# Unread products between the groups of rows while the first batch loads, and from the first microsecond

## Chip, cores, metric

One core of one Trainium2 chip. The metric is the device time of one execution in microseconds (us). Beside it, each execution has a span, the time from its first to its last instruction, and a mean granted clock of TensorE. The time is usually 2.1 to 2.2 us more than the span.

## The reference

Four batches of 6016 rows and 256 columns. A cross-covariance attention over the columns is followed by a gated feed-forward layer:

```python
qn = q / (norm(q, axis=1) + 1e-6);  kn = k / (norm(k, axis=1) + 1e-6)
s = kn.transpose(0, 2, 1) @ qn / tau           # 256 x 256 per batch
a = softmax(s)                                 # with 1e-9 added to the sum
x = (v @ a).reshape(24064, 256)
out = (sigmoid(x @ w_gate) * (x @ w_val)) @ w_out   # d_ff = 1536
```

The scores and norms of a batch need all of its rows, so nothing of the first batch's output can start before all of q and k of that batch are loaded.

## The kernel before

While the first batch loads, TensorE works group by group (four tiles of 128 rows; at the end a group of two tiles and one of one): score products, then the norms of the group before, which multiply squares by a column of ones.

```python
    def busy(n):

        ps = psg.tile([P, CH], FP32, tag="g", name="ps_busy")
        for _ in range(n):
            mm(ps[:, :P], ones_bf, ones_bf, True, True)

    ps_n0 = psm.tile([P, 2 * CB], FP32, tag="m", name="ps_n")
    sq = {}
    last0 = len(groups0) - 1
    for g in range(last0 + 2):
        if g <= last0:
            t0, nt = groups0[g]
            sq[g] = (
                squares(0, t0, nt, 0, nc.vector),
                squares(0, t0, nt, 1, nc.vector if g == last0 else nc.scalar),
            )
            for u in range(nt):
                score(0, t0, u)
        if g >= 1:
            norm_mms(ps_n0, sq.pop(g - 1), groups0[g - 1][1], g == 1, g == last0 + 1)
    st[0]["n"] = ps_n0
    norms_sqrt(0)
    # ... cut ...
    norms_inv(0)          # VectorE: r = r + 1e-6, r = 1 / r   (128x4)
    copy_s(0, 1)
    busy(12)
    spread_k(0)           # TensorE: ps_rk, needs r
    busy(10)
    # ... cut: scale, exponential, sums, products with the weights; then the main loop
```

`busy` was there already: products that nobody reads, between the stages of the softmax.

## Time and profile before

| | before |
|---|---|
| time, median of 3 | 840.12 us (839.49 to 840.18) |
| span of the profiled execution | 838.0 us |
| mean granted clock | 0.992 |
| TensorE busy | 817.0 us, 97% |

TensorE's busy share is that of an engine at its limit almost throughout. The clock rows, the chain of waits and the timeline of the head, which is where the change acts, are shown in the prediction below. In the chain, each line is a start, a length and what held the end there; a DMA line is a transfer waited for. In the windows, the columns are the window, its length, the busy time of TensorE, its weight load, VectorE, ScalarE and GpSimd, then clock, DMA share and GB/s.

### The profile page before, as it was taken

Reading aid. Unit: us, or ns where it says so; the run is one execution under the profiler, and the core shown is the slowest. Engines: PE = TensorE matmul, PEld = TensorE weight load, DVE = VectorE, ACT = ScalarE, POOL = GpSimd, SP = SyncE. Lnnn points to the kernel's source line nnn. Section 1 sums busy time; section 2 is a strip of 40 time slices with the busy share of each in tenths; the row PEclk is TensorE's granted clock in tenths of the full one; section 3 lists DMA queues with packets and bytes.
Section 4 is the critical chain, followed back from the end, with each engine's and each line's share of the span. In section 5 each row is a group of like instructions: output and inputs, shape, how many; then the busy total and the mean of one; then the engine's idle time right before and its main releaser. Section 6 shows DMA issues by size and latency. Waiting matters only on the chain.

```text
span 838.0 us, 14001 instructions
## 1 busy us (share of the span) xinstructions
PE 817.0 (97%) x5338; PEld 506.6 (60%) x5338; DVE 566.3 (68%) x977; ACT 390.6 (47%) x640; POOL 83.2 (10%) x159
## 2 busy tenths in 40 slices
PE   5899999999999999999999999999999999999998
PEld 4646666665666666665565666666566556665666
DVE  2377777776667777777656777777756666666664
ACT  4554444445644444444554444444654444444442
POOL 5532100002011100000210020000000000000000
PEclk9799999999999999999999999999999999999999
DMA  9999624226655443223864453223222422322211
GB/s 209 206 205 186 124 51 89 61 51 136 125 102 107 101 102 63 54 51 85 153 132 83 92 118 80 51 73 67 60 48 51 95 51 73 78 50 65 49 36 69
DMA packets 78739, 77.18 MB, mean 92 GB/s; under 512 B 50769, under 2 KB 55633, under 8 KB 78673
## 3 DMA queue, kind: packets, MB, share of 16 engines
q0 software_dynamic: 23920, 38.81, 28.0%
q1 hardware_dynamic: 54608, 36.97, 15.8%
q8 instruction: 41, 0.67, 0.3%
q10 hardware_dynamic: 144, 0.52, 0.2%
q14 instruction: 26, 0.20, 0.1%
HBM read 78.64 MB, written 24.64 MB: 123 GB/s over the span
## 4 chain that ended last, share of the span: by engine, by line
PE 91%; DMA 3%; DVE 2%; ACT 1%; issue 1%; POOL 0%; ACTq 0%; POOLq 0%
PE ps_o L88 29%; PE ps_gate L88 28%; PE ps_val L88 28%; PE ps_s L88 4%; DMA k_sb<-in_k_dram 3%; PE ps_gh L88 2%; DVE hT L351 1%; ACT g_sb L350 1%; PE ps_rk L88 0%; DVE out_sb L377 0%; ACT gh_H L306 0%; PE ps_n L88 0%; DVE gh_H L308 0%; DVE gh_G L308 0%; DVE x_sb L253 0%
## 5 line engine op out<-in xcount | busy, mean ns | idle before, releaser
L351 DVE TENSOR_TENSOR hT<-ps_val,g_sb 128x512 bf16<-128x512 f32 (+1 forms) x576 | 391.1, 679 | 219.9 <-ACT g_sb L350 216.3
L350 ACT ACTIVATE g_sb<-ps_gate 128x512 bf16<-128x512 f32 (+1 forms) x576 | 338.8, 588 | 399.8 <-PE ps_gate L88 387.3
L88 PE MATMUL ps_val<-vT,gh_H 128*128 128x512 bf16 (+1 forms) x1152 | 338.0, 375 | 0.5
L88 PE MATMUL ps_gate<-vT,gh_G 128*128 128x512 bf16 (+1 forms) x1152 | 337.5, 375 | 0.0
L88 PE MATMUL ps_o<-w_out_sb,hT 128*128 128x256 bf16 x2256 | 326.2, 273 | 0.0
L88 PEld LDWEIGHTS <-hT 128*128 128x128 bf16 x2256 | 220.7, 98 | 124.8
L88 PEld LDWEIGHTS <-gh_H 128*128 128x128 bf16 x1152 | 112.7, 98 | 132.9 <-ACT gh_H L306 1.5
L88 PEld LDWEIGHTS <-gh_G 128*128 128x128 bf16 x1152 | 112.5, 98 | 37.4 <-ACT gh_G L306 0.3
L377 DVE COPY out_sb<-ps_o 128x256 f32<-128x256 f32 x188 | 78.1, 415 | 20.9 <-PE ps_o L88 20.9
L106 POOL DMA_DIRECT2D v_sb<-in_v_dram x48 | 25.6, 534 | 631.7 <-DMA vT<-v_sb 466.0
L88 PE MATMUL ps_s<-k_sb,q_sb 128*128 128x256 bf16 x376 | 72.4, 296 | 13.1 <-ACT k_sb L128 6.8
L88 PEld LDWEIGHTS <-q_sb 128*128 128x128 bf16 x376 | 39.1, 104 | 20.8 <-issue 7.1
L169 DVE TENSOR_TENSOR sq<-q_sb 128x1024 bf16<-128x1024 bf16 (+3 forms) x46 | 30.4, 661 | 20.7 <-PE ps_n L88 17.4
L207 DVE TENSOR_TENSOR acc<-acc,sq 128x1024 bf16<-128x1024 bf16 (+1 forms) x66 | 44.2, 669 | 0.0
L97 POOL DMA_DIRECT2D q_sb<-in_q_dram x48 | 26.4, 549 | 15.6 <-DMA q_sb<-in_q_dram 5.5
L97 POOL DMA_DIRECT2D k_sb<-in_k_dram x48 | 26.1, 545 | 13.6 <-DMA k_sb<-in_k_dram 8.4
L169 DVE TENSOR_TENSOR sq<-k_sb 128x1024 bf16<-128x1024 bf16 (+2 forms) x34 | 22.4, 658 | 0.0
L167 ACT ACTIVATE sq<-k_sb 128x1024 bf16<-128x1024 bf16 (+1 forms) x12 | 12.2, 1021 | 15.6 <-DMA k_sb<-in_k_dram 12.6
L88 PE MATMUL ps_gh<-w_gate,e_sb 128*128 128x512 bf16 x48 | 14.1, 378 | 1.6 <-DVE rrow L281 1.2
L88 PE MATMUL ps_gh<-w_val,e_sb 128*128 128x512 bf16 x48 | 14.1, 379 | 0.4
L88 PEld LDWEIGHTS <-e_sb 128*128 128x128 bf16 x112 | 9.9, 97 | 6.8 <-issue 3.2
L306 ACT ACTIVATE gh_G<-ps_gh,rrow 128x512 bf16<-128x512 f32 x12 | 8.2, 687 | 9.7 <-PE ps_gh L88 9.6
(46 smaller groups left out, 101.6 us busy)
## 6 DMA issues: line engine op xcount, KB each, us to landing
out_dram<-out_sb SPq DMA_DIRECT2D x44, 512.0 KB, 2.8
v_sb<-in_v_dram POOLq DMA_DIRECT2D x44, 256.0 KB, 3.9
q_sb<-in_q_dram POOLq DMA_DIRECT2D x43, 256.0 KB, 6.3
k_sb<-in_k_dram POOLq DMA_DIRECT2D x43, 256.0 KB, 7.8
out_dram<-out_sb SPq DMA_DIRECT2D x4, 384.0 KB, 2.4
w_gate<-in_moe_w_gate_dram POOLq DMA_DIRECT2D x3, 256.0 KB, 6.9
w_val<-in_moe_w_val_dram POOLq DMA_DIRECT2D x3, 256.0 KB, 7.6
w_out_sb<-in_moe_w_out_dram POOLq DMA_DIRECT2D x1, 768.0 KB, 12.6
```

The source lines that it names most:

```text
L88: nc.tensor.matmul(out, lhsT=lhsT, rhs=rhs, start=start, stop=stop, **kw)
L97: nc.gpsimd.dma_start(out=tl[:, :nt, :], in_=rows(src, b)[:, t0 : t0 + nt, :])
L106: nc.gpsimd.dma_start(out=v_sb[:, :nt, :], in_=rows(v, b)[:, t0 : t0 + nt, :])
L167: nc.scalar.activation(out=sq[:, :nt, :], in_=src[:, :nt, :], func=ACT.Square)
L169: engine.tensor_tensor(out=sq[:, :nt, :], in0=src[:, :nt, :], in1=src[:, :nt, :], op=ALU.mult)
L207: nc.vector.tensor_tensor(out=acc[:, :nt, :], in0=acc[:, :nt, :], in1=st[b]["sq", w][:, :nt, :], op=ALU.add)
L306: nc.scalar.activation(out=dst, in_=ps, func=ACT.Copy, scale=r)
L350: nc.scalar.activation(out=g_sb[:, :n], in_=ps_gate[:, :n], func=ACT.Sigmoid)
L351: nc.vector.tensor_tensor(out=hts[b, ci][:, f, :n], in0=ps_val[:, :n], in1=g_sb[:, :n], op=ALU.mult)
L377: nc.vector.tensor_copy(out=out_sb[:, s, :], in_=ps)
```

## The change

The intent: in the kernel before, TensorE's granted clock falls from 1.00 to 0.50 at times (18.37 and 28.61 us in the windows of the prediction), and the engine waits for loads during the first 31 us. Unread products fill these waits, so that the real ones run at full clock.

```diff
+    busy(40)
     ps_n0 = psm.tile([P, 2 * CB], FP32, tag="m", name="ps_n")
 ...
         if g >= 1:
             norm_mms(ps_n0, sq.pop(g - 1), groups0[g - 1][1], g == 1, g == last0 + 1)
+        if g < NT // TPC:
+            busy(12)
     st[0]["n"] = ps_n0
```

`NT // TPC` is 11: one filling after each group of four tiles.

## The prediction

> **What bounds the kernel now.** I read the page first, then the chain of waits of the first 60 us, then the timeline of TensorE, then windows.
>
> ```profile
> PE 91%; DMA 3%; DVE 2%; ACT 1%; issue 1%; POOL 0%; ACTq 0%; POOLq 0%
> PEclk9799999999999999999999999999999999999999
> ```
>
> The chain that ended last is TensorE for 91% of the span, and the granted clock is full in every slice of 21 us but the second. From 60 us on TensorE is simply full of work that the diff doesn't touch. So only the head, some 40 us, can move, and what the head saves should arrive at the end undiminished. The chain of waits in the head:
>
> ```profile
> 10.92 10.63 DMA k_sb<-in_k_dram
> ...
> 21.84 9.74 DMA k_sb<-in_k_dram
> 31.57 0.04 issue
> 31.61 1.86 PE ps_s L88 x8
> 33.48 0.40 PE ps_n L88 x16
> 33.88 0.88 PE ps_s L88 x4
> 34.76 0.40 PE ps_n L88 x16
> 35.16 0.43 PE ps_s L88 x2
> 35.59 0.28 PE ps_n L88 x12
> 35.87 0.69 PE ps_busy L88 x12
> ```
>
> Columns are start, length, what. Up to 31.57 us the head is paced by the loads of q and k, whose queue is full; TensorE waits for them. At 31.57 us group 10, the last group of four rows, is there, and from then on nothing waits for a load: 4.26 us of TensorE work lead to 35.87 us. That is all that a better clock could shorten. The timeline of TensorE has the same work at two speeds:
>
> ```profile
> 26.61 1.03 PE L88 MATMUL ps_s<-k_sb,q_sb 128*128 128x256 bf16 x8 [0.55 <-DMA k_sb<-in_k_dram]
> 27.48 0.54 PE L88 MATMUL ps_n<-ones_bf,sq 128*128 128x1 bf16 x16
> ...
> 31.61 1.86 PE L88 MATMUL ps_s<-k_sb,q_sb 128*128 128x256 bf16 x8 [0.20 <-DMA k_sb<-in_k_dram]
> 33.27 0.61 PE L88 MATMUL ps_n<-ones_bf,sq 128*128 128x1 bf16 x16
> 33.74 1.01 PE L88 MATMUL ps_s<-k_sb,q_sb 128*128 128x256 bf16 x4
> 34.55 0.61 PE L88 MATMUL ps_n<-ones_bf,sq 128*128 128x1 bf16 x16
> ```
>
> From start to start, eight score products take 27.48 - 26.61 = 0.87 us (109 ns each) in the fast state and 33.27 - 31.61 = 1.66 us (208 ns each) in the slow one. The sixteen one-column products of the norms take 0.47 us slow (33.74 - 33.27) and about 0.41 us fast: hardly clock-bound.
>
> In quarter-microsecond windows the clock drops at 18.37 us, rises at 25.20, drops at 28.61 and rises at 35.44. The distances are 6.83, 3.41 and 6.83 us, so I cut the head into windows of 3.41 us on that grid:
>
> ```profile
> 11.54:14.96 3.42, 2.37 (x45) 2.10 (x44) 1.12 (x2) 1.49 (x2) 1.33 (x3) 1.00 1.12 210
> 14.96:18.37 3.41, 1.56 (x26) 1.43 (x26) 0.95 (x2) 1.15 (x2) 1.33 (x3) 1.00 1.12 208
> 18.37:21.78 3.41, 2.19 (x26) 1.64 (x25) 0.69 (x1) 1.09 (x2) 1.06 (x2) 0.50 1.12 210
> 21.78:25.20 3.42, 3.14 (x30) 2.29 (x29) 0.69 (x1) 1.93 (x2) 1.59 (x3) 0.50 1.12 209
> 25.20:28.61 3.41, 2.27 (x44) 2.06 (x43) 1.31 (x2) 1.11 (x2) 1.51 (x3) 1.00 1.12 210
> 28.61:32.03 3.42, 2.68 (x27) 1.97 (x27) 0.77 (x2) 1.41 (x2) 1.67 (x4) 0.50 1.19 200
> 32.03:35.44 3.41, 3.41 (x46) 2.64 (x45) 0.88 (x3) 1.33 (x2) 3.33 (x6) 0.50 1.21 207
> ```
>
> The third column is TensorE's busy time, the clock is the third from the end. A window with 2.37 us busy was followed by a fast one, those with 1.56 and 2.27 us by a slow one; from the slow state 3.14 and 3.41 us led out, 2.19 and 2.68 us did not. The last window, slow, is the stretch that counts.
>
> **What the Trainium skill says.** "TensorE: Matmul & The Clock Gate", Part 1, "What's actually happening": the default is half clock, a free-running window of about 3.4 us decides, and a busy window gives the full clock. The grid of 3.41 us and the steps between 1.00 and 0.50 agree. Its table lets the clock fall after an idle window; here it fell after windows that were 46% and 66% busy, so partial activity counts. Same page, "Back-to-back issue gap": 256 columns should take 213 ns cold and 109 ns warm; the trace has 208 and 109. The clock row reads 1.00 before any product ran, but the first sixteen score products (start 6.84 us, norms at 10.21 us) took 211 ns each, so that reading is only what stood before the first record.
>
> **The change part by part.** Nothing is removed or moved.
>
> 1. Forty products of 128 columns at the start. Their operand is filled by VectorE at 0.84 to 1.01 us; TensorE has nothing before 6.84 us. At half clock I estimate 107 ns each (half of 213 ns): 4.3 us, to about 5.4 us. They end before the first group can start, so they cost nothing. They make the first groups fast, but those then wait for loads all the same: worth nothing at the end by itself.
> 2. Twelve products after each of the eleven groups of four. The chain has 0.69 us for twelve in the fast state. A group then needs 0.87 + 0.41 + 0.69 = 1.97 us of TensorE, while groups arrive about every 2.5 us (waits end at 26.61, 29.15, 31.61 us). So ten of the eleven fillings end before the next group, and cost nothing.
> 3. The clock. Busy share becomes about 1.97/2.5 = 79%, some 2.7 us of a window, against 2.37 us that held and 2.27 us that did not. Should it fall, a group needs 1.66 + 0.47 + 12 x 0.107 = 3.41 us, more than arrives in, so TensorE saturates and the clock comes back. I take it that the tail is fast.
> 4. The tail. From 31.61 us: eight scores 0.87, norms 0.41, the eleventh filling 0.69, four scores 0.44 (half of 0.87), so the next norms start at 34.02 us, not 34.55 us: 0.53 us earlier. Without the filling it would be 1.2 us; the last filling is on the path, and gives over half away. After that VectorE must square the last row once these norms free its buffer, then the last norms follow: a chain of about 1.1 us with little clock in it (0.03 to 0.1 us faster). Sum: 0.55 to 0.65 us.
>
> Loads don't stop it: k of group 11 was issued at 24.38 us and took about 8.5 us (32.9 us), of group 12 at 27.09 plus 6.5 us (33.6 us); the new times ask for them at 33.6 and 34.4 us. Nor do weights: the first value weight, issued at 30.61 us plus the page's 7.6 us, is there at 38.2 us, and is wanted at 39.3 us instead of 39.93 us. So 840.12 - 0.6 = 839.5 us.
>
> **Rivals.**
> - The clock falls again, and the tail is slow with a filling in it: 12 x 0.107 = 1.28 us more, 841.4 us. For it: 2.7 us busy is not far above the edge, and the grid's phase may differ between runs. Against it: saturation heals it. Some 8%.
> - The gain is hidden by a load: the arrival of a late group or the value weight takes the place of the slow products. The time stays at 840.1 us. Margins of 0.7, 0.8 and 1.1 us speak against it, 10%.
> - The kernel before is sometimes fast in its tail already (its runs go from 839.49 to 840.18 us, the profiled one was 840.19): then the gain in the median is smaller, but the new time is the same.
> - A large gain, above 2% (17 us): there is no such thing to win, since the slow windows cost only 4.26 us minus about 2.5 us where no load is waited for.
>
> **Range and chances.** The centre is 839.5 us. Spread of the runs (0.7 us), the first rival and the size of the tail's gain make it 838.8 to 840.3 us. All outcomes lie within 0.2% of before, so within 2% is 0.99.
>
> **What would show it right or wrong.** Clock 1.00 from the first filling's second window to 36 us. Eight scores of group 10 in about 0.87 us, starting at 31.6 us as before, since loads pace it. Twelve fillings of about 0.69 us directly ahead of group 11's scores. First square root near 35.3 us in place of 35.91 us, and the same lead at the end. It is wrong if group 10 arrives at another time, if the tail is slow, or if a wait for a load stands between 33 and 41 us.

## More of the kernel before

GpSimd issues all loads that change the type, in this order: q and k of the first batch, a tile of v, six weight tiles, a tile of v, the output weights.

## The result, and the profile after

| | before | after |
|---|---|---|
| time, median of 6 | 839.64 us (839.29 to 840.18) | 839.49 us (839.43 to 839.55) |
| span, profiled | 838.0 us | 837.4 us |
| mean clock, profiled | 0.992 | 1.00 |

The ratio is 0.9997, 95% interval 0.9985 to 1.001. A ratio is the mean time of one kernel's runs over that of the other's of the same rounds, so it is not quite the ratio of the medians quoted. The spread is a seventh of what it was: 0.12 us against 0.89 us.

The clock row of the page after, in 40 slices of the span:

```profile
PEclk9999999999999999999999999999999999999999
```

The 7 in the second slice has gone. The chain of waits of the changed kernel, from the last load:

```profile
21.88 9.73 DMA k_sb<-in_k_dram
31.61 0.04 issue
31.66 1.03 PE ps_s L88 x8
32.69 0.38 PE ps_n L88 x16
33.07 0.69 PE ps_busy L88 x12
33.76 0.44 PE ps_s L88 x4
34.20 0.38 PE ps_n L88 x16
34.58 0.24 PE ps_s L88 x2
34.82 0.41 PE ps_n L88 x12
35.22 0.69 PE ps_busy L88 x12
```

The load ends where it ended before, at 31.6 us. The eight scores now take half as long, the eleventh filling stands in the chain with 0.69 us, and the last norms end at 35.22 us, against 35.87 us. The first square root starts at 35.26 us instead of 35.91 us. So 0.65 us were gained in the profiled pair, and the span is 0.6 us shorter. Yet the medians of the same session differ by 0.15 us only. The experiments ask why.

### The profile page after: what moved, and what is told of

Read it like the earlier page. It is cut to its first block, busy times and chain, and to the rows that moved or that the text cites. A ratio compares the mean times of both kernels' runs of the same rounds, so it can differ in the third digit from the quotient of the medians.

```text
span 837.4 us, 14334 instructions
## 1 busy us (share of the span) xinstructions
PE 821.7 (98%) x5499; PEld 514.2 (61%) x5510; DVE 566.4 (68%) x977; ACT 390.4 (47%) x640; POOL 83.0 (10%) x159
## 4 chain that ended last, share of the span: by engine, by line
PE 91%; DMA 3%; DVE 2%; ACT 1%; issue 1%; POOL 0%; ACTq 0%; POOLq 0%
PE ps_o L88 29%; PE ps_gate L88 28%; PE ps_val L88 28%; PE ps_s L88 4%; DMA k_sb<-in_k_dram 3%; PE ps_gh L88 2%; DVE hT L351 1%; ACT g_sb L350 1%; PE ps_rk L88 0%; DVE out_sb L377 0%; ACT gh_H L306 0%; PE ps_n L88 0%; DVE gh_H L308 0%; DVE gh_G L308 0%; DVE x_sb L253 0%
## 5 line engine op out<-in xcount | busy, mean ns | idle before, releaser
L88 PE MATMUL ps_s<-k_sb,q_sb 128*128 128x256 bf16 x376 | 66.2, 272 | 6.1 <-DMA k_sb<-in_k_dram 4.4
L88 PEld LDWEIGHTS <-q_sb 128*128 128x128 bf16 x376 | 36.6, 98 | 12.1 <-issue 5.6
L97 POOL DMA_DIRECT2D q_sb<-in_q_dram x48 | 26.4, 550 | 16.6 <-DMA q_sb<-in_q_dram 7.3
L88 PE MATMUL ps_busy<-ones_bf 128*128 128x128 bf16 x194 | 14.7, 234 | 1.1 <-DVE shift L125 1.1
```

What stands on the lines that cost most here:

```text
L88: nc.tensor.matmul(out, lhsT=lhsT, rhs=rhs, start=start, stop=stop, **kw)
L97: nc.gpsimd.dma_start(out=tl[:, :nt, :], in_=rows(src, b)[:, t0 : t0 + nt, :])
```

## The experiments

Twelve runs were made, each beside the kernel before. All results were correct.

| run | time, median | spans of its executions | mean clock |
|---|---|---|---|
| before_again | 840.10 | 837.2, 837.9, 838.0, 838.0, 838.7 | 0.987 to 0.991 |
| no_last_fill | 839.22 | 836.9, 837.1, 837.1, 837.1, 837.3 | 0.998 to 1.00 |
| start_only | 839.22 | 836.4, 836.8, 837.0, 837.1, 838.6, 838.8 | 0.988 to 0.992 |
| fills_only | 840.18 | 837.3, 837.9, 838.0, 838.0, 838.1 | 1.00 |
| after_again | 839.50 | 837.3, 837.3, 837.4, 837.9 | 1.00 |
| fills_only_2 | 840.09 | 837.8, 837.8, 838.1, 838.1 | 0.999 to 1.00 |
| double_last_fill | 840.50 | 838.2, 838.3, 838.4, 838.6 | 0.997 to 1.00 |
| wide_fills_no_last | 838.73 | 836.6, 836.8, 836.8, 837.0 | 0.999 to 1.00 |
| fills_only_root_in_psum | 840.02 | 837.2, 837.3, 837.3, 837.4, 837.4, 837.5 | 0.999 to 1.00 |
| wide_no_last_root_in_psum | 839.11 | 836.7, 836.8, 837.1, 837.2, 837.2, 837.4 | 0.999 to 1.00 |
| fills_of_four | 840.25 | 837.0, 837.3, 838.0, 838.2, 838.3, 838.4 | 0.993 to 0.998 |
| wide_fills | 839.81 | 837.4, 837.8, 837.9, 837.9, 837.9, 838.0 | 0.997 to 1.00 |

### The kernel before, again: before_again

No edit.

> The kernel before, unchanged, to see the clock and the time of each execution. Theory (the stretch from 31.6 us to the first square root is slow or fast by where the clock's 3.41 us windows happen to fall): times between 839.2 and 840.2 us that differ from execution to execution by 0.5 us or more, while the changed kernel kept within 0.12 us; executions with a lower mean clock tend to be the longer ones. Rival (the spread is chance of the loads, not of the clock): the times spread alike whatever the mean clock, and a kernel with a steady clock spreads alike.

Measured: with the executions of before that ran beside, 27 spans from 836.4 to 839.0 us. Eleven lie at or below 837.2 us, eleven at 837.9 to 838.1 us and five at 838.7 us or more, with none between. The mean clock does not sort them (838.7 us has 0.987, but 836.6 us has 0.989 in one execution and 0.994 in another), so that part of the theory fails; the mean counts all slow windows, while in the profiles those in the tail make the difference. The profiled execution of this run shows it. Its timeline of TensorE:

```profile
31.49 1.71 PE L88 MATMUL ps_s<-k_sb,q_sb 128*128 128x256 bf16 x8 [0.19 <-DMA k_sb<-in_k_dram]
33.03 0.54 PE L88 MATMUL ps_n<-ones_bf,sq 128*128 128x1 bf16 x16
33.44 0.60 PE L88 MATMUL ps_s<-k_sb,q_sb 128*128 128x256 bf16 x4
33.87 0.54 PE L88 MATMUL ps_n<-ones_bf,sq 128*128 128x1 bf16 x16
```

Same kernel, the load of group 10 only 0.12 us earlier, but the clock rises at 32.90 us in place of 35.44 us. The four scores take 0.43 us from start to start instead of 0.81 us, and the span is 837.2 us instead of 838.0 us, with a lower mean clock (0.990 against 0.992). The place of the clock's windows against the kernel differs between the two profiles, and that makes 0.7 of the 0.8 us between them. That it sorts all 27 executions is likely and not shown: only these two of the kernel before were profiled, and a held step of VectorE (below) can add 0.39 to 0.64 us too.

### Only the start: start_only

```diff
-        if g < NT // TPC:
-            busy(12)
```

> Only the forty products at the start. Theory (they warm the first groups, which wait for loads anyhow; the clock then falls between the groups as before): like the kernel before, 839.2 to 840.2 us with its spread, and with slow windows after some 10 us. Rival (the start is what counts: the clock, once up, stays up): 839.4 us or, as there is no last filling, 838.8 us, with little spread.

Measured: spans from 836.4 to 838.8 us, the spread of the kernel before, and a clock of 0.988 to 0.992. The start alone does not hold the clock. Its profiled execution has a bad placing of the windows:

```profile
35.73 1.44 PE L88 MATMUL ps_busy<-ones_bf 128*128 128x128 bf16 x12
36.96 1.14 PE L88 MATMUL ps_rk<-ident_f,r 128*128 128x128 f32 x4
```

Here the slow stretch goes on past the norms and takes in the old twelve fillings (1.44 us against 0.83 us) and the spreading of the roots (1.14 us against 0.68 us): 838.8 us.

### Only the fillings: fills_only and fills_only_2

```diff
-    busy(40)
```

> Only the fillings after the groups, none at the start. Theory (the fillings alone hold the clock, the start adds nothing to the end): 839.45 to 839.55 us, same spread as the changed kernel, clock 1.00 from about 12 us on. Rival (without a warm start the first groups fall behind their loads and never catch up): 0.3 us or more above the changed kernel, or a slow window in the tail.

Measured: the profiled execution has a span of 837.3 us and the same tail as the changed kernel, but the other four lie at 837.9 to 838.1 us, with a clock of 1.00. Neither side had expected that.

> The same kernel as in the run with the fillings alone, to see what four of its five executions did, whose span was 0.6 to 0.8 us above the profiled one at a clock of 1.00. Theory: the first groups run slow, so TensorE's instruction fetches (one packet of about 1 us on one of the 16 engines each, seen at 17, 25 and 34 us there) come at another time than with the start warmed, and in most executions one delays the keys of group 10 or 11 by 0.6 to 0.9 us: the profile, if it falls in such an execution, shows group 10 starting near 32.3 us at full clock. Rival: the tail itself is slow and the clock figure does not show it: 208 ns a score product after 31.6 us.

The profile fell in one (838.1 us), and both expectations are wrong: group 10 started at 31.68 us, at full clock. The time is lost after the tail. The timelines of GpSimd, VectorE and TensorE:

```profile
35.24 1.06 POOL L142 DMA_DIRECT2D w_out_sb<-in_moe_w_out_dram  x1
35.48 0.81 DVE L223 TENSOR_SCALAR r<-r 128x4 f32<-128x4 f32 x1 [0.17 <-ACT r L219]
36.65 0.68 PE L88 MATMUL ps_rk<-ident_f,r 128*128 128x128 f32 x4 [0.72 <-DVE r L224]
```

VectorE's step on four columns took 0.81 us instead of 0.17 us and ended at 36.29 us, as GpSimd's issue of the output weights did (36.30 us). TensorE then waited 0.72 us for the roots.

### The roots in PSUM: fills_only_root_in_psum

SBUF is the on-chip memory of the operands, PSUM the one that TensorE's products land in. The Trainium skill, "SBUF — State Buffer", section "Who interferes with whom", says that VectorE and GpSimd share a pair of SBUF ports, that a scalar step on SBUF operands may use it, and that issue order then decides who blocks. If so, the step should not wait when it reads PSUM (edit against fills_only):

```diff
-        nc.scalar.activation(out=s["r"], in_=s["n"], func=ACT.Sqrt)
+        nc.scalar.activation(out=s["n"], in_=s["n"], func=ACT.Sqrt)
...
-        nc.vector.tensor_scalar(out=r, in0=r, scalar1=1e-6, scalar2=None, op0=ALU.add)
+        nc.vector.tensor_scalar(out=r, in0=st[b]["n"], scalar1=1e-6, scalar2=None, op0=ALU.add)
```

> The fillings alone, with the square roots of the first norms written to PSUM, so that VectorE's small step on them (128x4) reads PSUM and not SBUF. In the second run of the fillings alone that step took 0.81 us in place of 0.17 us and ended with GpSimd's 1.06 us of issuing the output weights. Theory (VectorE waits there for the SBUF port that it shares with GpSimd): the step takes about 0.17 us whatever GpSimd does, span 837.2 to 837.5 us in all executions. Rival (the delay is something else, such as the instruction fetch): spans near 838.0 us in most executions as before.

Measured: all six spans at 837.2 to 837.5 us, where eight of nine had been at 837.8 us or more. The timelines of GpSimd and VectorE:

```profile
35.22 1.06 POOL L142 DMA_DIRECT2D w_out_sb<-in_moe_w_out_dram  x1
35.41 0.16 DVE L223 TENSOR_SCALAR r<-ps_n 128x4 f32<-128x4 f32 x1
```

The spans support the page. This profile alone does not: the step came 0.19 us after the issue began, and in fills_only, reading SBUF, it came 0.21 us after and was not held either; in fills_only_2, 0.24 us after, it was. So a step that comes 0.02 us sooner is a rival that the spans do not exclude. The profile of fills_only speaks against it. Inside the same issue (35.22 to 36.27 us) it has:

```profile
35.64 0.18 DVE L224 RECIPROCAL r<-r 128x4 f32<-128x4 f32 x1
35.73 0.39 DVE L247 COPY x_sb<-ps_s 128x256 f32<-128x256 f32 x1
```

They started 0.42 and 0.51 us after the issue did and took what they took outside it in fills_only_2 (0.18 and 0.39 us): a copy that reads PSUM is not held there, nor is every step on SBUF. Besides fills_only_2, the step on the roots was held in double_last_fill (0.56 us, to 36.85 us) and in fills_of_four (0.25 us, to 35.56 us), where a GpSimd issue ended at 36.86 and at 35.57 us. That the thing waited for is the port is the page's account; the runs show which step is held, and until when.

With the roots in PSUM, the fillings alone give the changed kernel's span (837.3 to 837.4 us), so the forty products do nothing for the end through the clock. As the kernel stands they matter all the same, since without them eight of nine executions were longer. In the profiles without them GpSimd's issue began at 35.22 to 35.24 us and the keys (k) of group 11 landed at 32.9 us; in the two of the changed kernel it was 35.40 and 35.41 us, and 33.2 us. There the step slipped by, once 0.07 us after that issue began and once 0.05 us ahead of it. Nobody had planned this.

The times of four executions were high by another 0.3 to 1.2 us beyond their spans; that is outside the program, and left aside.

### Without the last filling: no_last_fill

```diff
-        if g < NT // TPC:
+        if g < NT // TPC - 1:
             busy(12)
```

> The changed kernel without the filling after the eleventh group. Theory (that filling lies on the path at full length, 0.67 us): the four score products of the next group start up to 0.67 us earlier, but not before their keys land, about 33.2 us in the changed kernel's profile, so 0.35 to 0.67 us earlier; the time becomes 838.8 to 839.15 us, the clock stays at 1.00. Rival A (the clock falls without it): the tail is slow, 839.9 us or more. Rival B (a late load takes its place fully): 839.4 to 839.5 us.

Measured: 836.9 to 837.3 us, median 837.1 us; that is 0.25 us below the changed kernel's usual 837.35 us, less than the theory had. The profiled execution is the longest of the five (837.3 us). Its timeline of TensorE tells what took its place:

```profile
32.43 0.54 PE L88 MATMUL ps_n<-ones_bf,sq 128*128 128x1 bf16 x16
33.50 0.60 PE L88 MATMUL ps_s<-k_sb,q_sb 128*128 128x256 bf16 x4 [0.53 <-DMA k_sb<-in_k_dram]
```

Nothing stands between norms and scores any more, but the keys of group 11 came at 33.5 us, and TensorE waited 0.53 us for them. In the kernel before they had come at 32.9 us (issue at 24.38 us plus 8.5 us), here at 24.90 plus 8.6 us.

### Twice the last filling: double_last_fill

```diff
-            busy(12)
+            busy(24 if g == NT // TPC - 1 else 12)
```

> Twenty-four products in place of twelve after the eleventh group. Theory (that filling lies on the path at its full length): 0.67 us more than the changed kernel of the same call, span 838.0 us. Rival (the last squares or a load set the end there): 0 to 0.3 us more.

Measured: 838.2 to 838.6 us, which is 0.9 to 1.2 us above the changed kernel and more than the expected 0.67 us. Timelines of TensorE and VectorE:

```profile
33.09 1.50 PE L88 MATMUL ps_busy<-ones_bf 128*128 128x128 bf16 x24
36.29 0.56 DVE L223 TENSOR_SCALAR r<-r 128x4 f32<-128x4 f32 x1 [0.17 <-ACT r L219]
```

The filling takes 1.33 us from start to start (the scores follow at 34.42 us) in place of 0.67 us: the expected 0.66 us, all of it on the path. The rest of the profiled execution's 1.2 us is the held step again, 0.56 us instead of 0.17 us, which makes 0.39 us, and a last load that came 0.15 us later. The other three were not profiled.

### Wide fillings: wide_fills_no_last and wide_fills

Three products of 512 columns replace twelve of 128, ten replace the forty at the start: the same stream with a quarter of the instructions.

```diff
+    wide_bf = consts.tile([P, CH], BF16)
+    nc.vector.memset(wide_bf, 1.0)
...
+    def busy_wide(n):
+        ps = psg.tile([P, CH], FP32, tag="g", name="ps_busy")
+        for _ in range(n):
+            mm(ps, ones_bf, wide_bf, True, True)
...
-    busy(40)
+    busy_wide(10)
...
-        if g < NT // TPC:
-            busy(12)
+        if g < NT // TPC - 1:     # wide_fills: g < NT // TPC
+            busy_wide(3)
```

> Fillings of three products of 512 columns (the same stream, a quarter of the instructions), ten of them at the start, none after the eleventh group. Theory (fewer instruction fetches ahead of the last groups, so the keys of group 11 land at 32.9 us and not at 33.5 us, and no filling in the tail): the scores of group 11 start near 32.9 us, span 836.5 to 836.8 us, 0.5 to 0.9 us below the changed kernel, with a spread under 0.4 us. Rival A (the late keys have nothing to do with fetches): 837.1 us as without the last filling. Rival B (512 columns count less for the clock): slow windows.

Measured: 836.6 to 837.0 us, clock 0.999 to 1.00, time 838.73 us; the changed kernel had 837.3 to 837.9 us and 839.50 us, and no execution of the two overlaps. (Of the 0.77 us between the two times, 0.2 us lies outside the spans.) Against before the ratio is 0.9988, interval 0.9975 to 1.0001. The timeline of TensorE:

```profile
32.57 0.54 PE L88 MATMUL ps_n<-ones_bf,sq 128*128 128x1 bf16 x16
33.02 0.60 PE L88 MATMUL ps_s<-k_sb,q_sb 128*128 128x256 bf16 x4
```

The scores of group 11 follow the norms at once, as the keys were there at 33.0 us: the whole last filling is saved. By its spans this is the fastest version that also has a steady clock.

> Wide fillings after all eleven groups. Theory (what made the wide ones without the last faster is the missing last filling, 0.65 us): span 837.3 to 837.5 us, as the changed kernel. Rival (it is the smaller number of instructions and with it the fetches): 836.8 us as without the last.

Measured: the profiled execution had 837.4 us, as the theory said, the other five 837.8 to 838.0 us, above both expectations. None came near 836.8 us, so the width alone does not make the wide ones faster; leaving out the last filling does. Whether width helps there too, by letting the keys of group 11 land at 33.0 us and not at 33.5 us as in no_last_fill, rests on one profile each. The extra 0.5 us may be the held step (in the profiled one it came 0.19 us after GpSimd's issue began and took 0.17 us), but no profile caught it: not shown.

### Both together: wide_no_last_root_in_psum

The diffs of wide_fills_no_last and of the roots in PSUM together.

> Wide fillings, none after the eleventh group, and the roots in PSUM. Theory: as the wide fillings alone where the small step was not held up, span 836.6 to 836.9 us, times near 838.7 us; nothing more to gain from PSUM in most executions as the step came at 34.89 us, ahead of the issue of the output weights. Rival (the small step costs more from PSUM, or its read delays the next step): 0.1 to 0.3 us more.

Measured: two executions at 836.7 and 836.8 us, the profiled one among them, and four at 837.1 to 837.4 us, so the expectation was missed in most. The profiled execution has the step at 0.16 us, and every start of its tail as in wide_fills_no_last to 0.04 us. Why the four were longer stays open. With the roots in PSUM it should not be the held step; late keys, as in no_last_fill, would have the size.

### A third of the filling: fills_of_four

```diff
-            busy(12)
+            busy(4)
```

> Four products in place of twelve after each group, forty at the start. Busy time for a group is then 0.87 + 0.41 + 0.22 = 1.50 us of 2.5 us, some 2.05 us of a 3.41 us window. Theory (2.37 us held the clock in the kernel before, 2.27 us did not): the clock falls within some windows, mean clock 0.990 to 0.996, spans spread over 1 us or more. Rival (any regular filling holds it): clock 1.00 and span 836.9 us, as the last filling is 0.45 us shorter than in the changed kernel.

Measured: clock 0.993 to 0.998, spans from 837.0 to 838.4 us. So the clock fell, though less than expected in some executions. In the profiled one it fell at 17.4 us and rose at 20.8 us. Four products do not hold the clock and twelve do; where between them the edge lies was not tried.

### The changed kernel, again: after_again

No edit.

> The changed kernel, unchanged, on the chip of the runs beside it. Theory (a steady clock and the same loads): span 837.3 to 837.4 us in all executions, times near 839.5 us, unless this chip adds to the launch as some executions of the first batch showed. Rival (its small spread was luck, an instruction fetch can delay the last loads here too): some executions at a span near 838.0 us.

Measured: three executions at 837.3 to 837.4 us and one at 837.9 us; with those of the first comparison, nine of ten within 0.1 us and a mean of 837.40 us. The kernel before's 27 have a mean of 837.65 us. The rival has its one execution too; a held step would fit, but no profile shows it.

## Why the prediction was right, point by point

The time, 839.49 us for 839.5 us, is right, and the profile agrees step by step; the gain it was taken from is not what a reader should expect. There is luck in the base: the profiled execution had a slow tail, and the median of three, 840.12 us, happened to lie beside it (840.19 us). The same 0.6 us taken from the later median of six, 839.64 us, gives 839.04 us, below all six executions measured.

- **The start** (forty products, worth nothing at the end): right for the clock. They ended at 5.1 us and the first group began at 6.77 us, and without them, with the roots in PSUM, the spans were 837.2 to 837.5 us. It missed that they also shift GpSimd's issue: without them and with the roots in SBUF, eight of nine executions were at 837.8 us or more.
- **Fillings that cost nothing:** right for the ten. From the second on each had a wait for a load after it, 0.21 us or more, and after the first the second group began at once (8.31 us); the wait at 10.63 us took up what that cost.
- **The clock held:** right at twelve, and not at four, but the reason given, an edge between 2.27 and 2.37 us of busy time, does not stand. In the changed kernel's trace the clock record starts at 4.52 us, so its windows begin there and every 3.41 us after; those from 4.52 and 14.76 us had 1.75 and 2.08 us busy, and the clock held. In before_again it fell after 2.07 us. Two windows of start_only, the first followed by full clock, the second by half:

```profile
10.63:14.04 3.41, 2.23 (x40) 1.94 (x38) 1.39 (x2) 1.57 (x2) 1.39 (x3) 1.00 1.12 208
27.70:31.11 3.41, 2.22 (x44) 2.01 (x43) 0.88 (x2) 1.06 (x1) 1.25 (x3) 1.00 1.14 206
```

  What sorts them is the columns streamed by the products that start in a window: 256 for a score product, 128 for one of a filling, 1 for one of the norms. Fourteen score products of 256 columns and twenty of the norms started in the first, 3604 columns in all; ten and thirty-two in the second, 2592 columns. In the prediction's windows eleven score products (2848 columns) held and ten (2592) did not. Over the full-clock windows of the first 36 us in all fourteen traces, the clock fell after at most 2592 columns and held after at least 2848, if one product of 512 columns that is missing from the trace of wide_fills is counted. The changed kernel's lowest is 3472. No run was made to test this. (2.27 us is 67% of a window, not 66%.)
- **The tail:** right in each term. Scores 0.87 us (32.53 - 31.66), norms 0.40 us, filling 0.67 us, scores 0.43 us: the next norms start at 34.03 us, predicted 34.02 us. The root at 35.26 us, predicted near 35.3 us. The last filling on the path: shown by taking it away (0.25 us less with 128-column fillings, where late keys took over) and by doubling it (0.66 us more).
- **Loads don't stop it:** right, but with less to spare: the keys of group 11 came at 33.2 us (24.43 + 8.8), not 32.9 us, and without the last filling they did become the wait. That rival was underrated.
- **The rival of an uneven kernel before** was the one that came true. Eleven of 27 executions of before are faster than the changed kernel (836.4 to 837.2 us against 837.35 us); the one of them that was profiled has a fast tail without a filling in it. The others are 0.5 to 1.6 us slower. The change takes out the chance more than the time: the means of the spans differ by 0.25 us, and the ratio of the times is not told from one.
- **What the prediction did not have** is the held step: VectorE's step on the roots meets GpSimd's issue of the output weights, and lost 0.39 and 0.64 us in two profiles. In both profiles of the changed kernel it slips by.

## What to carry to other kernels

Before crediting a change of clock, run the unchanged kernel some ten times and look at where its slow windows fall: one profile is one throw. Filling belongs in waits, so end it one group before the last wait ends; a filling that no wait follows is paid in full, here 0.67 us of the 1.2 us that the clock gives. To ask whether a filling holds the clock, count the columns that it streams in a window too; here they sorted the windows, and TensorE's busy time did not. When work off the bound engine moves by a few tenths, look at which small VectorE steps it moves into a long GpSimd instruction.

## What the Trainium skill lacked or had wrong

- "TensorE: Matmul & The Clock Gate": its table has the clock fall after an idle window, and it tells of a clock that goes to and fro with short idle gaps, but gives no measure. Here it fell after windows that were 46% and 67% busy and, in another run, held after one of 51% (1.75 us). Busy time does not sort them; in fourteen traces the columns streamed do, at most 2592 of them before a fall and at least 2848 where the full clock held.
- The same page says that the window runs freely and counts the penalty as small. The runs show what it does to a measurement: 27 executions of one kernel from 836.4 to 839.0 us, with a gap from 837.2 to 837.9 us. Two executions of that kernel were profiled, and the place of the clock's windows makes 0.7 us between them.
- "SBUF — State Buffer", on who holds the shared port: the runs agree, 0.81 us in place of 0.17 us for a 128x4 step. It says that whoever issues first has the port for the whole instruction. Here, such steps that started up to 0.22 us after a GpSimd issue of 0.56 to 1.05 us began were not held, and those at 0.24, 0.31 and 0.48 us were, to the issue's end: the port seems not taken in the first 0.2 us. One at 0.80 us (in the kernel before) took 0.19 us and ended 0.04 us ahead of the issue.
- "Advanced Engine Details and Errata", section "ISA Cache", gives 16 KB or 256 instructions to a line of the instruction cache, but neither it nor another page says what a refill costs other transfers. In the kernel before, the list of DMA queues from 19 to 21 us has, for the instruction queue:

```profile
q8 instruction: 1, 0.02, 3.0%
```

  One packet of 16 KB, 3.0% of 16 engines in 2 us, so 0.96 us of one engine. The next keys landed at 21.55 us, 3.4 us after those before (18.18 us), where 2.5 us is usual. The changed kernel has a packet at 13.1 us, and its keys came at 13.1 and then 16.6 us. In all fourteen traces a gap of 3.4 to 3.9 us lies at the first such packet; the second one has a gap of 3.1 to 3.2 us in four, and none in the others. So the packet fits as the cause of the first gap, but no run tested it alone.
